# Attention in front of a dense layer: DMA transposes in and out, one score block over four banks, and v pooled by GpSimd, from pair 16 on

## The chip, the cores and the metric

The kernel runs on one core of one Trainium2 chip. The metric is the device time of one execution in microseconds (us). Every experiment is given as the median of its executions, and as a ratio to executions of the kernel before on the same chip in the same rounds.

The engines are PE (TensorE matmuls; PEld its weight loads), ACT (ScalarE), DVE (VectorE), POOL (GpSimd) and SP, whose queue here issues every DMA.

## The reference

Eight batches, eight heads, 576 tokens, head dimension 64. Two attentions are added: one over means of four tokens, one over a band of plus and minus three tokens. A dense layer with `h - tanh(h)` follows.

```python
q_d = q.reshape(B, H, Sd, 4, D).mean(axis=3)      # the same for k and v
out_d = sm_attn(q_d, k_d, v_d)                    # softmax attention, 144 x 144
out_up = np.repeat(out_d, 4, axis=2)
mask = np.abs(pos[:, None] - pos[None, :]) < 4
out_local = softmax(where(mask, q k^T / 8, -1e9)) @ v
x = (out_up + out_local) as [4608, 512]
h = x @ w_in                                      # 512 -> 2048
out = (h - tanh(h)) @ w_out                       # 2048 -> 512
```

## The kernel before

Heads are worked on in 32 pairs, four pairs to a batch. As soon as a batch has filled 512 more tokens of `xT`, a dense block (128 matmuls of 512 columns) can run; there are nine. The program lists operations with durations that it assumes, orders them by a list scheduler that prefers attention and fills PE with dense work, and writes each engine's instructions in that order. On the chip the order is fixed: **an engine that reaches an instruction too early stands still, whatever else is ready.** The waits of PE shown further down are such stops.

```python
def order(self): ...     # list scheduling with the assumed ns and latencies
LAT = {"PE": 270, "ACT": 150, "DVE": 110, "POOL": 150, "SP": 50, "DMA": 1800}
```

The parts that the change touches, cut to the core (`ts` and `ox` are two PSUM banks each, `px` is `ox` seen as bf16):

```python
# q and k: PE transposes for early pairs, a DMA transpose from pair T_DMA = 14 on
op("SP", 700, dma_start_transpose(qT[s] <- qr[s]), pri=pri)
op("DMA", 2500, None, ...)
op("ACT", 600, A.copy(full[:, i] <- qT[s][:, i]))          # twice
# scores in two blocks, each with its exponentials, both in ts
op("PE", 420, s1, writes=ts)                     # 8 matmuls of the band
op("ACT", 870, exp(e1 <- ps)); op("DVE", 700, e1 *= mask)
op("PE", 380, s2, writes=ts)                     # 2 of the band, 4 pooled
op("ACT", 240, exp(e2v <- ps)); op("ACT", 560, exp(e3 <- ps)); op("DVE", 220, e2v *= mask)
# pooling v on PE for two pairs, in ox, then a cast on ACT
op("PE", 750, six matmuls pick x vw, writes=["ox"]); op("ACT", 490, vd <- ox)
# outputs, normalisation, transposes back, join
op("PE", 570, outs, writes=ox)
op("DVE", 200, reciprocal); op("DVE", 1010, ln[s] <- po * r)
op("PE", 370, back, writes=ox)                   # 7 transposes
op("ACT", 190, od <- px[1]); op("DVE", 680, xT <- px[0] + od)
```

The softmax here doesn't subtract the row's maximum and nothing guards it: scores larger than these inputs give would overflow.

## Time and profile before

| what | number | where it is read |
|---|---|---|
| PE busy | 334.3 of 357.4 us | page, part 1 |
| last join of attention | 253 us, so 104 us of dense work alone follow | groups of the join's line |
| dense matmuls | start to start 216 ns; 1152 of them are 249 us | PE timeline |
| transposes back; pooling of v | 0.37 us per pair; 0.70 per two pairs | PE timeline |
| ACT busy, 140 to 220 us | 86% | windows |

The median was 362.01 us over three executions (361.08 to 363.34); the profiled one took 359.08 us, of which 357.4 us are the span.

This is the head of the page of the kernel before: busy time and share of the span by engine, then the busy share in tenths in 40 slices of 8.9 us.

```profile
span 357.4 us, 6978 instructions
PE 334.3 (94%) x2646; PEld 173.1 (48%) x2692; DVE 219.4 (61%) x362; ACT 236.2 (66%) x406; POOL 123.9 (35%) x156
PE   7777999999999999999999999989999999999995
ACT  3686987688864988888888899974343443434421
DMA  8999999999999999798788925200100010010012
```

PE is nearly always busy, and after slice 28, where attention is over, it alone is. But busy PE time must be read with care. The Trainium skill, "Trainium Kernel Development and Optimization", section "Performance Expectations", calls matmul busy time a bad metric, because matmuls are pipelined. This trace agrees: a dense matmul is shown as 379 ns long, yet starts follow each other every 216 ns. So PE work is costed here by the spacing of starts. These rows are from the PE timeline of the kernel before (start, length, line, operation, count): transposes back, the first score block, four dense matmuls, then pooling of v and the second score block.

```profile
191.85 0.22 PE L525 MATMUL ps_ox<-ident,ln_102 128*128 128x128 bf16 x1
191.91 0.22 PE L526 MATMUL ps_ox<-ident,ln_102 128*128 128x128 bf16 x1
191.97 0.42 PE L529 MATMUL ps_ox<-ident,ln_102 120*128 120x120 bf16 x5
192.32 0.38 PE L449 MATMUL ps_ts<-qk_90 64*128 64x120 bf16 x8
192.64 1.04 PE L581 MATMUL ps_hy_529<-w_out_sb,gT_106 128*128 128x512 bf16 x4
...
194.38 0.72 PE L361 MATMUL ps_ox<-vw_82,pick 128*128 128x256 bf16 x5
194.94 0.27 PE L363 MATMUL ps_ox<-vw_82,pick 128*128 128x256 bf16 x1
195.15 0.22 PE L449 MATMUL ps_ts<-qk_90 64*128 64x96 bf16 x2
195.20 0.29 PE L464 MATMUL ps_ts<-qkd_95 64*128 64x144 bf16 x4
195.42 0.82 PE L581 MATMUL ps_hy_529<-w_out_sb,gT_106 128*128 128x512 bf16 x3
```

From 191.85 to the next start of other work is 0.47 us for the transposes back (0.37 where nothing delays it), and pooling takes from 194.38 to 195.15, 0.77 us (six times its usual spacing of 113 ns is 0.68).

Finally what PE itself waited for between 130 and 265 us (PE instruction, releaser, us in total, times, longest; the first three of 13 lines), and the busy times of all engines from 140 to 220 us:

```profile
PE ps_ts L449 <- ACT qk_91 L404: 1.8, 4, 0.6
PE ps_ts L449 <- ACT E_97 L472: 0.8, 2, 0.6
PE ps_ox L498 <- DVE E_98 L487: 0.5, 1, 0.5
```

```profile
core 0: us, PE busy (x) PEld busy (x) DVE busy (x) ACT busy (x) POOL busy (x), PEclk, DMA share, GB/s
140.00:220.00 80.00, 76.51 (x682) 40.67 (x691) 60.93 (x99) 68.81 (x111) 39.52 (x44) 1.00 0.82 165
```

PE waits before the first score block, for the copies of q and k on ACT (L404). ACT is 86% busy there (68.81 of 80).

### The profile page before, as it was taken

How to read it: one execution, taken by the hardware profiler on the slowest of the kernel's cores; microseconds unless marked ns; L12 is line 12 of the kernel's file. 1: busy time of each engine (PE TensorE's matmuls, PEld its weight loads, DVE VectorE, ACT ScalarE, POOL GpSimd, SP SyncE). 2: the span in 40 equal slices, each digit the busy share in tenths (PEclk: the TensorE clock that was granted, in tenths of full speed). 3: DMA queues.
4: the chain of work that ended last, by engine and by line, in shares of the span. 5: the costliest groups of instructions: out<-in, count | busy, mean ns of one | idle time of the engine just before them, and what ended most of it. 6: DMA issues, size and time to landing. Idle time of an engine off the chain costs nothing.

```text
span 357.4 us, 6978 instructions
## 1 busy us (share of the span) xinstructions
PE 334.3 (94%) x2646; PEld 173.1 (48%) x2692; DVE 219.4 (61%) x362; ACT 236.2 (66%) x406; POOL 123.9 (35%) x156
## 2 busy tenths in 40 slices
PE   7777999999999999999999999989999999999995
PEld 3454455555545454545555454445444444444442
DVE  5786775869976576867887778676443334434300
ACT  3686987688864988888888899974343443434421
POOL 7654666576542346444654446420000000000000
PEclk9899999999999999999999999999999999999999
DMA  8999999999999999798788925200100010010012
GB/s 199 226 390 304 258 253 253 212 235 273 242 217 165 214 184 227 172 171 176 155 211 184 214 64 97 64 0 31 56 34 29 29 61 30 29 61 29 29 67 82
DMA packets 86128, 52.94 MB, mean 148 GB/s; under 512 B 65103, under 2 KB 77391, under 8 KB 86095
## 3 DMA queue, kind: packets, MB, share of 16 engines
q1 hardware_dynamic: 86094, 52.50, 66.3%
q8 instruction: 21, 0.34, 0.4%
q14 instruction: 13, 0.10, 0.1%
HBM read 37.74 MB, written 9.44 MB: 132 GB/s over the span
## 4 chain that ended last, share of the span: by engine, by line
PE 65%; ACT 11%; DMA 10%; DVE 6%; issue 5%; POOL 2%; SPq 1%; POOLq 0%; ACTq 0%; DVEq 0%
PE ps_hy_530 L581 7%; PE ps_hy_530 L554 7%; PE ps_hy_529 L554 7%; PE ps_hy_528 L554 7%; PE ps_hy_527 L581 7%; PE ps_hy_529 L581 7%; PE ps_hy_527 L554 6%; PE ps_hy_528 L581 5%; ACT qk_91 L404 4%; DMA vst_80<-in_v_dram 3%; DMA qkn_73<-in_q_dram 3%; ACT qk_90 L404 2%; PE ps_ox L498 2%; DMA vst_81<-in_v_dram 2%; PE ps_ox L361 2%
## 5 line engine op out<-in xcount | busy, mean ns | idle before, releaser
L554 PEld LDWEIGHTS <-w_in_sb 128*128 128x128 bf16 x576 | 52.7, 98 | 58.8 <-issue 2.2
L581 PEld LDWEIGHTS <-gT_105 128*128 128x128 bf16 x320 | 29.2, 98 | 31.6
L581 PEld LDWEIGHTS <-gT_106 128*128 128x128 bf16 x256 | 23.8, 98 | 27.6
L431 POOL TENSOR_TENSOR half<-qk_91 128x576 f32<-128x576 bf16 x16 | 19.2, 1203 | 34.5 <-ACT qk_91 L404 26.4
L431 POOL TENSOR_TENSOR half<-qk_90 128x576 f32<-128x576 bf16 x14 | 16.1, 1149 | 37.6 <-ACT qk_90 L404 31.7
L404 ACT COPY qk_90<-qT_92 128x576 bf16<-128x576 bf16 x18 | 21.0, 1180 | 0.0
L404 ACT COPY qk_91<-qT_93 128x576 bf16<-128x576 bf16 x18 | 20.7, 1188 | 0.0
L581 PE MATMUL ps_hy_527<-w_out_sb,gT_105 128*128 128x512 bf16 x78 | 20.4, 379 | 0.2 <-issue 0.2
L581 PE MATMUL ps_hy_528<-w_out_sb,gT_105 128*128 128x512 bf16 x78 | 20.3, 379 | 0.3 <-issue 0.3
L581 PE MATMUL ps_hy_529<-w_out_sb,gT_105 128*128 128x512 bf16 x75 | 20.1, 379 | 0.3
L581 PE MATMUL ps_hy_530<-w_out_sb,gT_105 128*128 128x512 bf16 x77 | 19.4, 379 | 0.3 <-issue 0.2
L515 DVE TENSOR_TENSOR ln_101<-ps_ox,r_99 128x896 bf16<-128x896 f32 x16 | 17.4, 1089 | 0.4
L472 ACT ACTIVATE E_97<-ps_ts 128x960 bf16<-128x960 f32 x16 | 15.8, 988 | 1.9 <-PE ps_ts L449 1.9
L581 PE MATMUL ps_hy_530<-w_out_sb,gT_106 128*128 128x512 bf16 x63 | 16.7, 379 | 0.3 <-issue 0.2
L581 PE MATMUL ps_hy_527<-w_out_sb,gT_106 128*128 128x512 bf16 x62 | 16.7, 379 | 0.0
L581 PE MATMUL ps_hy_528<-w_out_sb,gT_106 128*128 128x512 bf16 x60 | 16.1, 379 | 0.3 <-issue 0.2
L581 PE MATMUL ps_hy_529<-w_out_sb,gT_106 128*128 128x512 bf16 x61 | 16.0, 379 | 0.1
L475 DVE TENSOR_TENSOR E_97<-E_97,mask 128x960 bf16<-128x960 bf16 x16 | 13.5, 844 | 3.5 <-ACT E_97 L472 3.2
L515 DVE TENSOR_TENSOR ln_102<-ps_ox,r_100 128x896 bf16<-128x896 f32 x14 | 15.2, 1088 | 0.4
L472 ACT ACTIVATE E_98<-ps_ts 128x960 bf16<-128x960 f32 x14 | 13.7, 976 | 2.4 <-PE ps_ts L449 1.7
L475 DVE TENSOR_TENSOR E_98<-E_98,mask 128x960 bf16<-128x960 bf16 x16 | 13.5, 844 | 2.1 <-ACT E_98 L472 2.1
L554 PE MATMUL ps_hy_527<-xT_66,w_in_sb 128*128 128x512 bf16 x35 | 13.3, 380 | 1.4 <-DVE xT_69 L534 1.2
(220 smaller groups left out, 867.2 us busy)
## 6 DMA issues: line engine op xcount, KB each, us to landing
out_dram<-y_110 SPq DMA_DIRECT2D x12, 256.0 KB, 2.3
out_dram<-y_111 SPq DMA_DIRECT2D x12, 256.0 KB, 3.0
out_dram<-y_112 SPq DMA_DIRECT2D x12, 256.0 KB, 2.1
qkn_72<-in_q_dram SPq DMA_DIRECT2D x8, 288.0 KB, 7.3
qkn_72<-in_k_dram SPq DMA_DIRECT2D x8, 288.0 KB, 7.3
qkn_73<-in_q_dram SPq DMA_DIRECT2D x8, 288.0 KB, 4.7
qkn_73<-in_k_dram SPq DMA_DIRECT2D x8, 288.0 KB, 5.5
qkn_74<-in_q_dram SPq DMA_DIRECT2D x8, 288.0 KB, 6.7
```

Source lines behind the costliest of these rows:

```text
L361: T.matmul(pv[:, 0, :], pick[:, t, :], vw[w][:, :, t, 0:64], start=(t == 0), stop=(t == NT - 1))
L404: op("ACT", 600, lambda i=i: A.copy(out=full[:, i].rearrange("p (g a) -> p g a", a=A6), in_=qT[s][:, i].rearrange("p a g -> p g a")), read ...
L431: eng.tensor_tensor(out=half, in0=four[:, :, :, 0:2], in1=four[:, :, :, 2:4], op=ALU.add)
L472: op("ACT", 870, lambda: A.activation(out=e1, in_=ps[:, :, 0:480], func=AF.Exp, scale=SCALE), reads=ts, writes=[("E", s, 0)], pri=pri)
L475: op("DVE", 700, lambda: V.tensor_tensor(out=e1, in0=e1, in1=mask[:, 0:480].unsqueeze(1).to_broadcast([128, 2, 480]), op=ALU.mult), reads= ...
L498: T.matmul(po[:, hh, 65 * t:65 * t + 65], E[s][:, c:c + 128], vw[w][:, 2 * jj + hh, t, :], start=True, stop=True)
L515: op("DVE", 1010, lambda: V.tensor_tensor(out=ln[s].rearrange("p n (h d) -> p h n d", d=D), in0=blocks[:, :, :, 0:64], in1=r[s].unsqueeze( ...
L554: T.matmul(ps_hy[slot], w_in_sb[:, dc, fc * 128:(fc + 1) * 128], xT[dc][:, kb * 512:kb * 512 + 512], start=(dc == 0), stop=(dc == N_DC - 1))
L581: T.matmul(ps_hy[slot], gT[g][:, fc, ts * 128:ts * 128 + 128], w_out_sb[:, fc, :], start=(fc == 0), stop=(fc == N_FF - 1))
```

## The change

From pair 16 on: v is pooled by two additions on GpSimd, from a second load of v in rows of four tokens; the scores are one PE block over the four banks of `ts` and `ox`; the outputs go back through a DMA transpose, and DVE or GpSimd joins the two attentions in SBUF. DMA transposes of q and k start at pair 16, not 14, come first in the DMA queue and are planned as shorter. The v buffers go from 6 to 5 to make room. Some smaller parts of the diff also touch earlier pairs (padding of `E` and `qkd`, one of the seven transposes back on 16 rows instead of 128).

```diff
-    NQKN, NVST, NVW = 4, 6, 3
+    NQKN, NVST, NVW = 4, 5, 3
+    v4 = fixed("v4", [72, 2, 2, 4 * D], FP32, 2)
+    vp = fixed("vp", [72, 2, 2, D + 1], BF16, 2)
+    lT = fixed("lT", [128, 7, 128], BF16, 2)
     ...
+        op("POOL", 1150, a1, reads=[("v4", s)], writes=["v2"], pri=10 * p - 12)
+        op("POOL", 750, a2, reads=["v2"], writes=[("vp", s)], pri=10 * p - 12)
     ...
-               writes=[("qT", s), ("qTq", s)], pri=pri)
-            op("DMA", 2500, None, ...
+               writes=[("qT", s), ("qTq", s)], pri=-50)
+            op("DMA", 1300, None, ...
     ...
+        if new:
+            op("PE", 620, s12, reads=qks + [("qkd", s)], writes=ts + ox, pri=pri)
     ...
+        if p >= X_DMA:
+            op("SP", 600, lambda: nc.sync.dma_start_transpose(
+                out=lT[s], in_=ln[s].rearrange("p n c -> p (n c)")), ..., pri=-50)
+            ...                                # the planned DMA, the definition of join
+            P.choice([("DVE", 850, lambda: join(V)), ("POOL", 1450, lambda: join(GP))],
+                     reads=[("lT", s)], writes=[("x", b, j)], pri=pri)
+            return
     ...
-    M2_FIRST, T_DMA = 16, 14
+    M2_FIRST, T_DMA, X_DMA, NEW = 16, 16, 16, 16
```

More of the change, by code (lines that the diff above doesn't have):

```diff
@@ L193 @@
     mask = fixed("mask", [128, 576], BF16)
-    warm = fixed("warm", [128, 512], BF16)
     xT = [fixed(f"xT{j}", [128, NTOK], BF16) for j in range(NP)]
@@ L205 @@
     half = fixed("half", [128, 2, G, 2], FP32)
-    qkd = fixed("qkd", [128, 2, G], BF16, 2)
-    E = fixed("E", [128, 1728], BF16, 2)
+    qkd = fixed("qkd", [128, 344], BF16, 2)
+    v4 = fixed("v4", [72, 2, 2, 4 * D], FP32, 2)
+    v2 = fixed("v2", [72, 2, 2, 2 * D], FP32)
+    vp = fixed("vp", [72, 2, 2, D + 1], BF16, 2)
+    E = fixed("E", [128, 1840], BF16, 2)
+    lT = fixed("lT", [128, 7, 128], BF16, 2)
+    warm = lT[0].rearrange("p n c -> p (n c)")[:, 0:512]
     r = fixed("r", [128, 2, 7], FP32, 2)
@@ L351, in prep_v, with load_v4, issue, pool_v4 @@
                  writes=[("vw", w, jj)], pri=10 * p - 12)
+    def load_v4(p):
+        b, h0, s = p // NP, 2 * (p % NP), p % 2
+        src = v[b, h0]
+        def issue():
+            nc.sync.dma_start(
+                out=v4[s].rearrange("p h w c -> p (h w) c"),
+                in_=bass.AP(tensor=src.tensor, offset=src.offset,
+                            ap=[[4 * D, 72], [72 * 4 * D, 4], [1, 4 * D]]))
+        load(700, issue, [("v4", s)], 1100, -30)
+    def pool_v4(p):
+        s = p % 2
+        def a1():
+            GP.tensor_tensor(out=v2, in0=v4[s][:, :, :, 0:128],
+                             in1=v4[s][:, :, :, 128:256], op=ALU.add)
+        def a2():
+            GP.tensor_tensor(out=vp[s][:, :, :, 0:64], in0=v2[:, :, :, 0:64],
+                             in1=v2[:, :, :, 64:128], op=ALU.add)
+        op("POOL", 1150, a1, reads=[("v4", s)], writes=["v2"], pri=10 * p - 12)
+        op("POOL", 750, a2, reads=["v2"], writes=[("vp", s)], pri=10 * p - 12)
     def pool_v(hb):
@@ L399, in attention @@
                reads=[("qr", s, 0), ("qr", s, 1)],
-               writes=[("qT", s), ("qTq", s)], pri=pri)
-            op("DMA", 2500, None, reads=[("qTq", s), ("qr", s, 0), ("qr", s, 1)],
+               writes=[("qT", s), ("qTq", s)], pri=-50)
+            op("DMA", 1300, None, reads=[("qTq", s), ("qr", s, 0), ("qr", s, 1)],
                writes=[("qT", s)], pri=pri)
@@ L435, in add2 @@
             with nc.allow_low_precision("pooled q and k"):
-                eng.tensor_tensor(out=qkd[s], in0=half[:, :, :, 0],
+                eng.tensor_tensor(out=qkd[s][:, 0:2 * G].rearrange("p (i g) -> p i g", i=2),
+                                  in0=half[:, :, :, 0],
                                   in1=half[:, :, :, 1], op=ALU.add)
@@ L444, in attention, with score @@
         sc = ps.rearrange("p n c -> p (n c)")
-        def score(t, hh, c):
+        def score(t, hh, c, sc=sc):
             rows = slice(64 * hh, 64 * hh + 64)
@@ L455, in s1, with s2 @@
                     score(t, hh, 512 * hh + QW * t)
-        def s2():
+        def s2(sc=sc, step=16):
             for hh in range(2):
-                score(4, hh, 512 * hh)
+                score(4, hh, 512 * hh, sc)
             for i in range(2):
@@ L463, in s2, with s12 @@
                     c = 512 * hh + 96 + G * i
-                    T.matmul(sc[:, c:c + G], qkd[s][rows, 1, 16 * i:16 * i + 128],
-                             qkd[s][rows, 0, :], start=True, stop=True)
+                    k0 = G + step * i
+                    T.matmul(sc[:, c:c + G], qkd[s][rows, k0:k0 + 128],
+                             qkd[s][rows, 0:G], start=True, stop=True)
+        def s12():
+            s1()
+            s2(po.rearrange("p n c -> p (n c)"), 72)
         qks = [("qk", s, i) for i in range(2)]
         yield
-        op("PE", 420 * cold, s1, reads=qks, writes=ts, pri=pri)
+        new = p >= NEW
+        ps2, ts2 = (po, ox) if new else (ps, ts)
+        if new:
+            op("PE", 620, s12, reads=qks + [("qkd", s)], writes=ts + ox, pri=pri)
+        else:
+            op("PE", 420 * cold, s1, reads=qks, writes=ts, pri=pri)
         e1 = E[s][:, 0:960].rearrange("p (h c) -> p h c", h=2)
@@ L479, in attention @@
         yield
-        op("PE", 380 * cold, s2, reads=qks + [("qkd", s)], writes=ts, pri=pri)
+        if not new:
+            op("PE", 380 * cold, s2, reads=qks + [("qkd", s)], writes=ts, pri=pri)
         op("ACT", 240, lambda: A.activation(
-            out=e2v, in_=ps[:, :, 0:96], func=AF.Exp, scale=SCALE),
-           reads=ts, writes=[("E", s, 1)], pri=pri)
+            out=e2v, in_=ps2[:, :, 0:96], func=AF.Exp, scale=SCALE),
+           reads=ts2, writes=[("E", s, 1)], pri=pri)
         op("ACT", 560, lambda: A.activation(
-            out=e3, in_=ps[:, :, 96:384], func=AF.Exp, scale=SCALE / 16.0),
-           reads=ts, writes=[("E", s, 2)], pri=pri)
+            out=e3, in_=ps2[:, :, 96:384], func=AF.Exp, scale=SCALE / 16.0),
+           reads=ts2, writes=[("E", s, 2)], pri=pri)
         op("DVE", 220, lambda: V.tensor_tensor(
@@ L500, in outs @@
                 for half in range(2):
-                    c = 1152 + 288 * hh + 16 * half
+                    c = 1152 + 288 * hh + 128 * half
                     o = 65 * (NT + half)
                     for i in range(2):
+                        vv = vp[s][:, hh, i, :] if new else vd[w][:, i, 2 * jj + hh, :]
                         T.matmul(po[:, hh, o:o + 65],
-                                 E[s][:, c + G * i:c + G * i + 128],
-                                 vd[w][:, i, 2 * jj + hh, :],
-                                 start=(i == 0), stop=(i == 1))
+                                 E[s][0:vv.shape[0], c + G * i:c + G * i + 128],
+                                 vv, start=(i == 0), stop=(i == 1))
         P.fresh.add(len(P.ops))
         op("PE", 570 * cold, outs,
-           reads=[("E", s, 0), ("E", s, 1), ("E", s, 2), ("vw", w, jj), ("vd", w)],
+           reads=[("E", s, 0), ("E", s, 1), ("E", s, 2), ("vw", w, jj),
+                  ("vp", s) if new else ("vd", w)],
            writes=ox, pri=pri)
@@ L525, in back @@
             T.transpose(px[1][:, 0:128], ln[s][:, 5, :], ident)
-            T.transpose(px[1][:, 16:144], ln[s][:, 6, :], ident)
+            T.transpose(px[1][:, 128:144], ln[s][0:16, 6, :], ident[0:16, 0:16])
             for t in range(NT):
@@ L530, in back, with join @@
                             ident[0:n, 0:n])
+        if p >= X_DMA:
+            op("SP", 600, lambda: nc.sync.dma_start_transpose(
+                out=lT[s], in_=ln[s].rearrange("p n c -> p (n c)")),
+               reads=[("ln", s)], writes=[("lT", s), ("lTq", s)], pri=-50)
+            op("DMA", 1000, None, reads=[("lTq", s), ("ln", s)],
+               writes=[("lT", s)], pri=pri)
+            pool = lT[s][:, 5:7, :].rearrange("p n c -> p (n c)")[:, 0:G]
+            def join(eng):
+                x0 = xT[j][:, b * S:b * S + 480]
+                eng.tensor_tensor(
+                    out=x0.rearrange("p (t g a) -> p t g a", t=4, a=4),
+                    in0=lT[s][:, 0:4, 0:QW].rearrange("p t (g a) -> p t g a", a=4),
+                    in1=pool[:, 0:120].rearrange("p (t g) -> p t g", t=4)
+                    .unsqueeze(3).to_broadcast([128, 4, 30, 4]), op=ALU.add)
+                x1 = xT[j][:, b * S + 480:(b + 1) * S]
+                eng.tensor_tensor(
+                    out=x1.rearrange("p (g a) -> p g a", a=4),
+                    in0=lT[s][:, 4, 0:96].rearrange("p (g a) -> p g a", a=4),
+                    in1=pool[:, 120:144].unsqueeze(2).to_broadcast([128, 24, 4]),
+                    op=ALU.add)
+            P.choice([("DVE", 850, lambda: join(V)), ("POOL", 1450, lambda: join(GP))],
+                     reads=[("lT", s)], writes=[("x", b, j)], pri=pri)
+            return
         op("PE", 370 * cold, back, reads=[("ln", s)], writes=ox, pri=pri)
@@ L651 @@
            writes=[("vd", i)], pri=-96)
+    for i in range(2):
+        op("DVE", 70, lambda i=i: V.memset(E[i][:, 1728:1840], 0.0),
+           writes=[("E", i, 2)], pri=-94)
     op("DVE", 1200, c_pick, reads=["group"], writes=["pick"], pri=-95)
@@ L692 @@
     made = 0
+    for i in range(2):
+        op("DVE", 70, lambda i=i: V.memset(qkd[i][:, 288:344], 0.0),
+           writes=[("qkd", i)], pri=-94)
+        op("DVE", 70, lambda i=i: V.memset(vp[i][:, :, :, 64:65], 4.0),
+           writes=[("vp", i)], pri=-94)
     work = [attention(p) for p in range(NPAIR)]
@@ L697 @@
     for p in range(NPAIR):
-        if p % 2 == 0:
+        if p % 2 == 0 and p < NEW:
             pool_v(p // 2)
@@ L710 @@
         load_next()
+        if NEW <= p + 1 < NPAIR:
+            pool_v4(p + 1)
+        if NEW <= p + 3 < NPAIR:
+            load_v4(p + 3)
         if p % NP == NP - 1:
```

## The prediction

> **What bounds the kernel now.** TensorE. The page gives PE 334.3 of 357.4 us busy. After the last attention pair (last join at 252 us) only dense work is left, four matmuls per 0.86 us (chain of waits): 105 us of the 9 dense blocks is a pure PE tail. At pair 16 (about 132 us) some 300 of 1152 dense matmuls are done and 512 are ready, so PE has filler throughout. Attention pace (about 7.3 us per pair, DMA queue's timeline) matters only where PE waits in order for it. The waits show some 7.5 us of PE idle between 120 and 250 us. ACT (85 to 90% busy, windows) and the DMA engines (share about 0.95 from 120 to 200) stand close behind.
>
> **What goes, per pair from 16 on**, by spacing in the PE timeline rather than busy time, which overlaps:
> - transposes back: seven matmuls, 0.37 us
> - pooling v on PE: 0.70 us per two pairs, 0.35
> - two score blocks (0.32 and about 0.28) become one; three interruptions of dense work vanish, some of which cost 0.1 to 0.2 us ("issue" waits before weight loads). I put 0.15 here.
>
> So 0.87 us per pair, 14 us over 16 pairs, all on the bounding engine. Pairs 14 and 15 return to PE transposes: plus 1.2 us. ACT loses the 0.29 us copy of od and half of vd's 0.59 us cast per pair, about 9 us, and some slow copies (1.18 to 0.64 us): another 2 us.
>
> **What comes.** POOL: two additions on 72 partitions, by elements from the present 1.2 and 0.75 us ones, about 1.7 us per pair; POOL is half idle. The join takes SBUF inputs, about 0.75 us on DVE as before. The Trainium skill, "SBUF — State Buffer", section "SBUF: two separate sides", says GpSimd and a DVE operation with two SBUF inputs block each other on a shared port pair; the trace agrees: the same mask product takes 0.64 to 1.19 us. More of that, off the critical path. DMA, per pair: 295 KB more loads (estimate 1 us of 16 engines) and an output transpose (a present one takes about 2.1 us of 16 engines from 220 to 240 us, 4.6 us to landing; the new one estimate 1.7): share 1.0 to 1.2, as at 60 to 100 us. SP works in order and transposes hold it 1.25 to 3.1 us each, so loads queue longer. The four-bank score block must wait until the previous pair's normalisation frees its banks: score, exponentials (2.0 us), outputs, normalisation (1.3) plus queueing, an estimated 7 to 8 us loop, about today's pace.
>
> **Net.** Attention ends at 252 to 262 us, equal or slightly later, with more dense work done by then; the backlog never runs out. Gain 14, less 1.2, less a little for new in-order PE waits: 12.5, so 349.5 us, range 343 to 356. Chances: faster by over 2% 0.77, same 0.18, slower 0.05.
>
> **Right if:** PE idle from 130 to 260 us stays under 10 us; the tail after the last join shrinks to 85 to 95 us; attention PE work per pair falls from 1.95 to about 1.15 us; POOL busy grows by 25 to 30 us; landing of input transposes rises to 5 to 6 us.
>
> **Wrong if:** the DMA queue sets the pace and PE stands at the score blocks waiting for late input transposes (over 1 us per pair), or the bank loop exceeds 9 us per pair, or the shorter v prefetch (5 buffers) delays the DMA-bound first 70 us.

## The result, and the profile after

The changed kernel took 348.24 us (median of four, 346.70 to 348.94) against 361.77 (four), a ratio of 0.961 with a 95% interval of 0.957 to 0.966. Executions over 1.5% slower than the fastest of the same kernel are left out of the means. The predicted 349.5 us was 1.3 us off. Its page:

```profile
span 346.3 us, 6847 instructions
PE 328.0 (95%) x2556; PEld 163.5 (47%) x2556; DVE 223.8 (65%) x362; ACT 224.8 (65%) x382; POOL 169.9 (49%) x210
PE   6787989999999999999999999899999999999995
ACT  4585886768978768787878778599753434343411
DMA  8999999999999998999999999645231000100021
```

PE stays full, GpSimd gains 46 us, and the DMA engines are busy to slice 25, not 23, and nearer to full from slice 17 on. The PE timeline around one pair shows one score block in place of two:

```profile
195.70 0.39 PE L478 MATMUL ps_ts<-qk_88 64*128 64x120 bf16 x8
195.92 0.21 PE L478 MATMUL ps_ox<-qk_88 64*128 64x96 bf16 x2
195.97 0.29 PE L494 MATMUL ps_ox<-qkd_93 64*128 64x144 bf16 x4
196.19 0.39 PE L619 MATMUL ps_hy_539<-xT_65,w_in_sb 128*128 128x512 bf16 x1
```

It takes 0.49 us from its first start to the next dense matmul. Then PE's waits from 130 to 265 us and the same stretch of busy times as before:

```profile
PE ps_ox L538 <- DVE E_100 L527: 1.5, 3, 0.7
PE ps_ox L538 <- DVE E_100 L514: 0.4, 2, 0.2
PE ps_ox L538 <- DVE E_101 L514: 0.4, 1, 0.4
```

```profile
140.00:220.00 80.00, 77.78 (x610) 37.83 (x609) 62.72 (x90) 61.27 (x96) 62.39 (x72) 1.00 1.13 233
```

The waits for ACT before the score blocks are gone. In their place PE now waits inside the output block (L538) for the mask products on DVE (L514, L527). ACT fell from 68.81 to 61.27 us, POOL rose from 39.52 to 62.39, and the DMA share from 0.82 to 1.13.

**An account of PE.** I split the span of each profiled execution into PE work and PE idle. Work is the number of weight loads of a kind (all are recorded, some matmuls are not) times the usual spacing of starts of that kind: 216 ns for a dense matmul (and for the 28 warming ones at the start), 54 for a transpose back, 113 for one of pooling, 32 in an output block, 43 for an input transpose, 23 on average for scores, which start in twos 4 ns apart. The 216 ns agrees with the Trainium skill, "TensorE: Matmul & The Clock Gate", section "Wait — 56ns, not 53.3ns?", which gives 215.7 ns for 512 columns. Idle is the rest; it holds the start (15 us of the first 30), what a reduced clock costs, and 4 us at the end.

| profiled execution | span | PE work | of it back / pooling / input transposes | PE idle | idle, late | last join at |
|---|---|---|---|---|---|---|
| before | 357.4 | 313.8 | 12.1 / 10.8 / 7.2 | 43.6 | 21.6 | 253.1 |
| after | 346.3 | 303.3 | 6.0 / 5.4 / 8.3 | 42.9 | 17.4 | 260.9 |

So 10.5 of the 11.1 us between these two executions is PE work that is no longer done. Idle from 130 us on fell from 18.5 to 13.7 us, and idle before that rose from 25.1 to 29.2; in this run the clock was lower in the first slices, 0.83 against 0.91 in the first 20 us. The medians differ by 13.5 us; the profiled execution of the kernel before was one of its fast ones, and the 2.4 us in between lie within its own spread.

The column "idle, late" leaves out a part that only blurs the comparison. In all fourteen profiles PE's first 850 weight loads are of the same kinds in the same order, and yet PE idle up to there, 94 to 99 us into the span, runs from 22.0 us (before) to 27.6 us; it is 25.5 us in the changed kernel. "Idle, late" is the idle time after these 850. It fell by 4.2 us, so with 10.5 us of work the change is worth 14.7 us after that point, against 13.5 by the medians. Whether the smaller v buffer has a part in the idle time before it was not tested.

### The profile page after: what moved, and what is told of

Same layout as the page of the kernel before. It is cut to its first block, busy times and chain, and to the rows that moved or that the text cites. A ratio compares the mean times of both kernels' runs of the same rounds, so it can differ in the third digit from the quotient of the medians.

```text
span 346.3 us, 6847 instructions
## 1 busy us (share of the span) xinstructions
PE 328.0 (95%) x2556; PEld 163.5 (47%) x2556; DVE 223.8 (65%) x362; ACT 224.8 (65%) x382; POOL 169.9 (49%) x210
## 4 chain that ended last, share of the span: by engine, by line
PE 69%; DVE 10%; ACT 9%; issue 3%; DMA 3%; POOL 2%; SPq 1%; ACTq 0%; POOLq 0%; DVEq 0%
PE ps_hy_540 L646 8%; PE ps_hy_538 L619 8%; PE ps_hy_539 L619 7%; PE ps_hy_541 L646 7%; PE ps_hy_538 L646 7%; PE ps_hy_539 L646 6%; PE ps_hy_540 L619 6%; PE ps_hy_541 L619 6%; PE ps_ox L538 3%; DVE qr_87 L416 2%; PE ps_ts L478 2%; DMA qkn_73<-in_k_dram 2%; PE ps_ox L545 2%; PE ps_ts L442 2%; PE ps_ox L389 2%
## 5 line engine op out<-in xcount | busy, mean ns | idle before, releaser
L646 PEld LDWEIGHTS <-gT_110 128*128 128x128 bf16 x320 | 30.2, 98 | 34.5
L646 PEld LDWEIGHTS <-gT_111 128*128 128x128 bf16 x256 | 24.0, 98 | 27.4
L646 PE MATMUL ps_hy_539<-w_out_sb,gT_110 128*128 128x512 bf16 x80 | 20.7, 379 | 0.0
L646 PE MATMUL ps_hy_540<-w_out_sb,gT_110 128*128 128x512 bf16 x80 | 20.4, 379 | 0.0
L646 PE MATMUL ps_hy_538<-w_out_sb,gT_110 128*128 128x512 bf16 x80 | 20.4, 379 | 0.0
L646 PE MATMUL ps_hy_541<-w_out_sb,gT_110 128*128 128x512 bf16 x80 | 20.1, 379 | 0.0
L432 ACT COPY qk_89<-qT_91 128x576 bf16<-128x576 bf16 x16 | 18.7, 1193 | 0.0
L432 ACT COPY qk_88<-qT_90 128x576 bf16<-128x576 bf16 x16 | 18.4, 1188 | 0.0
L556 DVE TENSOR_TENSOR ln_106<-ps_ox,r_104 128x896 bf16<-128x896 f32 x16 | 17.4, 1090 | 0.5
L646 PE MATMUL ps_hy_540<-w_out_sb,gT_111 128*128 128x512 bf16 x64 | 16.9, 379 | 0.0
L646 PE MATMUL ps_hy_541<-w_out_sb,gT_111 128*128 128x512 bf16 x64 | 16.8, 379 | 0.0
L646 PE MATMUL ps_hy_539<-w_out_sb,gT_111 128*128 128x512 bf16 x64 | 16.6, 379 | 0.0
L646 PE MATMUL ps_hy_538<-w_out_sb,gT_111 128*128 128x512 bf16 x64 | 16.4, 379 | 0.0
L514 DVE TENSOR_TENSOR E_101<-E_101,mask 128x960 bf16<-128x960 bf16 x16 | 13.1, 820 | 3.9 <-ACT E_101 L511 3.7
L514 DVE TENSOR_TENSOR E_100<-E_100,mask 128x960 bf16<-128x960 bf16 x16 | 13.6, 847 | 2.8 <-ACT E_100 L511 2.8
```

Source lines behind the costliest of these rows:

```text
L432: op("ACT", 600, lambda i=i: A.copy(out=full[:, i].rearrange("p (g a) -> p g a", a=A6), in_=qT[s][:, i].rearrange("p a g -> p g a")), read ...
L514: op("DVE", 700, lambda: V.tensor_tensor(out=e1, in0=e1, in1=mask[:, 0:480].unsqueeze(1).to_broadcast([128, 2, 480]), op=ALU.mult), reads= ...
L556: op("DVE", 1010, lambda: V.tensor_tensor(out=ln[s].rearrange("p n (h d) -> p h n d", d=D), in0=blocks[:, :, :, 0:64], in1=r[s].unsqueeze( ...
L646: T.matmul(ps_hy[slot], gT[g][:, fc, ts * 128:ts * 128 + 128], w_out_sb[:, fc, :], start=(fc == 0), stop=(fc == N_FF - 1))
```

## The experiments

Theory: PE always has dense work ready, so the time is PE work plus PE idle, and 0.71 us of work per pair left PE. Rivals: (A) the 11 us taken off ACT did it; (B) the other order of issue, with its waits, did it.

| run | edit of the changed kernel | median, us | ratio to before (95%) | PE work | PE idle | idle, late | last join |
|---|---|---|---|---|---|---|---|
| (after) | none | 348.2 | 0.961 (0.957 to 0.966) | 303.3 | 42.9 | 17.4 | 260.9 |
| x_pe_back | outputs back by PE | 355.5 | 0.981 (0.974 to 0.989) | 309.4 | 44.7 | 18.5 | 273.2 |
| old_scores_pool | scores and pooling as before | 360.6 | 0.993 (0.983 to 1.002) | 308.8 | 51.7 | 24.8 | 242.0 |
| pe_dose | 12.5 us of empty PE work | 357.3 | 0.986 (0.978 to 0.995) | 315.9 | 39.3 | 14.6 | 269.4 |
| act_dose | 9 us of empty ACT work | 348.4 | 0.963 (0.955 to 0.971) | 303.3 | 43.1 | 18.6 | 261.0 |
| scores_only | v pooled on PE | 352.6 | 0.974 (0.965 to 0.982) | 308.8 | 41.8 | 15.9 | 251.5 |
| gp_pool_only | scores in two blocks | 352.1 | 0.972 (0.964 to 0.980) | 303.3 | 47.2 | 21.4 | 255.8 |
| pace_dose | 20 us more on GpSimd | 358.1 | 0.987 (0.978 to 0.996) | 303.3 | 52.5 | 26.4 | 270.9 |
| hints_back | planning figures as before | 354.7 | 0.978 (0.969 to 0.988) | 303.3 | 47.1 | 24.5 | 270.2 |
| less_dma | second v load almost gone (wrong result) | 358.7 | 0.987 (0.980 to 0.995) | 303.3 | 53.7 | 27.5 | 258.2 |
| all12 | all but the input transposes from pair 12 | 355.1 | 0.980 (0.973 to 0.986) | 300.5 | 52.6 | 26.4 | 273.0 |
| join_dve | joins on DVE only | 345.6 (344.3 without a slow one) | 0.950 (0.941 to 0.959) | (slow run) | | | |
| join_dve_again | the same kernel | 346.3 | 0.957 (0.952 to 0.962) | 303.3 | 42.3 | 16.3 | 260.2 |

All were correct but less_dma. The kernel before took 361.4 to 362.3 us (medians of fast executions) beside these runs. Work, idle and last join are those of each profiled execution. Against the changed kernel, work and late idle together differ by what the medians differ by, to about 1 us, in every row that has them (old_scores_pool: 5.5 and 7.4 us, by the medians 12.4); total idle does so less well.

### Is it PE, or ACT?

**x_pe_back** puts the transposes back on PE.

```diff
-    M2_FIRST, T_DMA, X_DMA, NEW = 16, 16, 16, 16
+    M2_FIRST, T_DMA, X_DMA, NEW = 16, 16, 32, 16
```

> The changed kernel with the output transposes put back on PE (seven matmuls and a copy on ACT per pair, no output DMA). Theory (the time is PE work plus PE idle, and PE has a backlog of dense work): 16 pairs x 0.37 us = 6 us come back, 354 us (352 to 356), with PE work by counts and spacing 6 us up on the changed kernel. Rival A (the gain came from ACT, which lost 11 us): 16 x 0.29 us of copies come back, at most 4.6 us and less, as ACT is no longer full. Rival B (the gain is the fewer in-order waits or the new order of issue): no change beyond 2 us.

It gave 355.5 us, 7.3 more, with 6.1 us more work and 1.8 us more idle. Rival A allows at most 4.6.

**pe_dose** and **act_dose** add work to one engine and leave the order alone.

```diff
         def outs():
+            if new:                            # ahead of the output matmuls
+                junk = po[:, 0].bitcast(BF16)
+                for z in range(14):
+                    T.transpose(junk[:, 128 * (z % 4):128 * (z % 4) + 128], ident, ident)
```

> The changed kernel with 14 transposes of the identity added ahead of the output matmuls of each pair from 16 on, overwritten afterwards, in unchanged order on every engine: about 14 x 0.053 = 0.75 us of PE work per pair, 12 us in all, nothing on any other engine. Theory: 12 us slower, 360 us (358 to 362). Rivals A and B: PE has room, so it takes at most half, 354 us or less.

```diff
+        def exp3():
+            A.activation(out=e3, in_=ps2[:, :, 96:384], func=AF.Exp, scale=SCALE / 16.0)
+            if new:
+                for z in range(2):
+                    A.copy(out=od[s], in_=ps2[:, z, 96:240])
```

> The changed kernel with two copies of 144 elements from PSUM (0.29 us each) added on ACT after the third exponential of each pair from 16 on, order unchanged: 16 x 0.58 = 9.3 us more on ACT, as much as the change took off it. Theory: ACT is off the critical path, 348 to 350 us. Rival A: most of 9 us comes back, 354 to 358 us.

The dose on ACT cost nothing clear of the noise (348.4 us): rival A falls. The dose on PE cost 9.1 us, less than the 12 expected and 0.7 us under the range given, but well over the rivals' 6. The account says why: work rose by 12.5 us, and idle fell by 3.6 (late idle by 2.8), because PE came later to the waits in the output blocks and found the mask products done: by spacing PE lost 0.3 us there, against 4.2 in the changed kernel. So in this run a microsecond of PE work cost 0.73 us.

### Scores and pooling

**old_scores_pool** undoes both.

```diff
-    M2_FIRST, T_DMA, X_DMA, NEW = 16, 16, 16, 16
+    M2_FIRST, T_DMA, X_DMA, NEW = 16, 16, 16, 32
```

> The changed kernel with the scores in two blocks and v pooled on PE as before, output and input transposes by DMA. Theory: 16 x 0.34 us of pooling on PE and 16 x about 0.1 us of a further block come back, 7 us, so 355 us (353 to 357). Rival A: 8 casts of 0.59 us, at most 4.7 us. Rival B: less than 2 us. A fourth possibility, that the wait of the four-bank block for its banks costs something, would make this smaller than 7 us.

It cost 12.4 us by the medians where 7 were expected. Work rose by 5.5 as foreseen; idle by 8.8 (late idle by 7.4), which was not. So two runs split the pair, with separate thresholds for the two parts:

```diff
+    M2_FIRST, T_DMA, X_DMA, NEW, NEWV = 16, 16, 16, 16, 32     # scores_only
+    M2_FIRST, T_DMA, X_DMA, NEW, NEWV = 16, 16, 16, 32, 16     # gp_pool_only
```

> Score blocks merged from pair 16 on as in the change, but v pooled on PE as before (no second load of v); transposes as in the change. Undoing scores and pooling together cost 12 us, of which 5.5 is PE work of pooling and 9 is PE idle. Theory 1 (the merged block is what removed the idle, by fewer interruptions and one wait instead of two): only the 5.4 us of pooling come back, PE idle stays within 2 us of the changed kernel's 43: 353 to 355 us. Theory 2 (pooling on PE, with its wait for the banks of the outputs and its cast on ACT, makes the idle): 358 to 361 us.

> v pooled by GpSimd from the second load as in the change, but the scores of pairs 16 on in two blocks over two banks as before. PE work as in the changed kernel (303 us). Theory 1: PE idle rises by 6 to 9 us, 354 to 357 us. Theory 2: idle stays near 43 us, 348 to 350 us. If both give about half, the two act together.

With merged scores and pooling on PE (scores_only), the 5.5 us of pooling are back and idle is no higher: 352.6 us, 0.4 under the range of theory 1. With GpSimd pooling and two score blocks (gp_pool_only), work is that of the changed kernel, but idle is 4.3 us up (late idle 4.0): 352.1 us, between the ranges of the two theories. So **pooling on GpSimd pays through work, the merged score block through idle**. By spacing, the time lost between dense matmuls and a score block after 130 us was 6.2 us before, 4.9 in gp_pool_only, and 1.5 in both kernels with merged blocks. Alone the two are worth 4.4 and 3.9 us, undone together 12.4; the missing 4 us are idle of old_scores_pool, where PE waited 4.4 us at score blocks for ACT's copies of q and k. Why these waits are longer there than in gp_pool_only was not settled.

That run also shows that an early end of attention does not make a fast kernel: with the last join earliest of all, at 242.0 us, it is the slowest, while the changed kernel ends attention 7.8 us later than the kernel before and is 13.5 us faster.

### Pace, plan and waits

**pace_dose** doubles the first GpSimd addition and tells the plan so.

```diff
-        op("POOL", 1150, a1, reads=[("v4", s)], writes=["v2"], pri=10 * p - 12)
+        op("POOL", 2400, a1_twice, reads=[("v4", s)], writes=["v2"], pri=10 * p - 12)
```

> The changed kernel with the first GpSimd addition of the pooling of v done twice (1.27 us more on GpSimd per pair, 20 us in all), and told so to the ordering, which so plans attention slower: attention gets slower, PE work is the same. Theory (PE has a backlog of dense work, so attention pace is off the critical path as long as the order of PE's instructions expects it): last join 5 to 20 us later, time within 3 us of 348. Rival (attention pace bounds): 355 us or more.

358.1 us: my expectation failed. PE work was the same, idle 9.6 us higher. But the waits do not say that attention's pace bounds; 9.0 of the 12.0 us that PE waits from 130 to 275 us are for mask products:

```profile
PE ps_ox L541 <- DVE E L530: 6.4, 9, 1.5
PE ps_ox L541 <- DVE E L517: 2.6, 2, 2.2
```

And the mask products themselves were slower, though nothing was added to DVE. Groups of DVE from 130 to 260 us (count, busy us, mean ns, idle before and its releaser), first the changed kernel, then pace_dose:

```profile
L514 DVE TENSOR_TENSOR E_100<-E_100,mask 128x960 bf16<-128x960 bf16 x8 | 7.6, 956 | 2.1 <-ACT E_100 L511 2.0
L514 DVE TENSOR_TENSOR E_101<-E_101,mask 128x960 bf16<-128x960 bf16 x8 | 6.9, 857 | 2.9 <-ACT E_101 L511 2.8
L527 DVE TENSOR_TENSOR E_100<-E_100,mask 128x192 bf16<-128x192 bf16 x8 | 3.7, 462 | 0.0
```

```profile
L517 DVE TENSOR_TENSOR E<-E,mask 128x960 bf16<-128x960 bf16 x15 | 19.0, 1268 | 7.4 <-ACT E L514 7.4
L530 DVE TENSOR_TENSOR E<-E,mask 128x192 bf16<-128x192 bf16 x15 | 9.2, 611 | 0.0
```

The large product went from 907 ns (mean of 956 and 857) to 1268, the small one to 611. That is what the Trainium skill, "SBUF — State Buffer", section "SBUF: two separate sides", describes: a GpSimd instruction that reads SBUF and a DVE instruction with two SBUF inputs hold a shared port pair in turn. The traces agree. In the fourteen profiles together, the 150 products of this size that no GpSimd instruction overlapped took 0.64 to 0.66 us, all of them; the others took up to 3.76 us. After 130 us, 12 of 16 are overlapped in pace_dose (mean 1.42 us) and 13 of 16 in the changed kernel (0.97 us). So a dose on GpSimd is not only a change of pace; this run does not test what it was made for.

**less_dma** was to test the pace without touching an engine.

```diff
+            if p >= NEW + 2:
+                nc.sync.dma_start(out=v4[s][:, 0, 0, 0:64], in_=...)   # a sixteenth of the row
+                return
-        load(700, issue, [("v4", s)], 1100, -30)
+        load(700 if p < NEW + 2 else 300, issue, [("v4", s)], 1100 if p < NEW + 2 else 100, -30)
```

> The changed kernel with the second load of v cut to a sixteenth from pair 18 on (pairs 18 and up then pool old values: a wrong result on purpose) and the ordering told that it is cheap. Frees the saturated DMA queue by an estimated 1 us per pair: a clean test of attention pace, which touches no engine's work. Rival (attention pace bounds the time): last join some 10 us earlier and time down by 5 us or more. Theory (PE has backlog; pace is off the path): last join earlier, 245 to 258 us, time within 2.5 us of 348.

Both theories missed: 358.7 us, with less DMA and the same work. Attention was hardly faster (last join 258.2 us; input transposes every 8.0 us against 8.6), so the pace was not what was bought. The plan, told that a load is cheap, had changed the order, so this run is no clean test of pace either. By spacing PE lost 10.7 us at and in the output blocks after 130 us, against 4.2 in the changed kernel, again with waits for the mask products. DVE came to them later: from pair 18 on the large product began 1.20 us after its exponentials on average, against 0.54 us. What in the order did that was not followed up.

**hints_back** changes the order alone.

```diff
-               writes=[("qT", s), ("qTq", s)], pri=-50)
-            op("DMA", 1300, None, ...
+               writes=[("qT", s), ("qTq", s)], pri=pri)
+            op("DMA", 2500, None, ...
```

> The changed kernel with the planning figures of the input transposes put back (2500 ns and the pair's priority in the DMA queue, instead of 1300 ns and the first place): the same instructions in another order. Theory: the same PE work, so within 3 us of 348, any difference being PE idle. Rival B (the gain is in the order): 353 us or more.

354.7 us, more than the 3 us that I allowed: rival B holds in part. The same instructions in another order cost some 6 us (4.2 us of idle in the profiled execution, 7.1 of late idle; it was the fastest of its four). Part of it may be clock: in that execution, after waits of 0.72 and 0.96 us, the granted clock stood at 0.50 from 213.9 to 220.7 us, and the other three had a lower mean clock still (0.971 to 0.975, against 0.990). Not run was the other side: the kernel before with the new planning figures alone. So, as far as these runs show, the gain needs the work removed **and** an order that fits.

### More of it, and a repair

**all12** starts outputs, scores and pooling at pair 12.

```diff
-    M2_FIRST, T_DMA, X_DMA, NEW = 16, 16, 16, 16
+    M2_FIRST, T_DMA, X_DMA, NEW = 16, 16, 12, 12
```

> The changed kernel with output transposes, merged scores and GpSimd pooling from pair 12 on instead of 16 (input transposes by DMA still from 16). Theory: 4 more pairs lose 0.37 + 0.34 us of PE work, 2.9 us, and some idle; against it stands that the DMA engines are at a share of 1.2 there and that less dense work is ready: 345 to 348 us. If DMA sets the pace there and PE has no backlog, 350 us or more with PE idle up between 80 and 130 us.

Work fell by 2.8 us as expected, but the time rose to 355.1 us: the expectation failed. The added idle is not between 80 and 130 us, where I had looked for it, but just after. Windows of this run:

```profile
136.00:140.00 4.00, 3.56 (x28) 1.46 (x26) 4.00 (x4) 4.00 (x6) 3.92 (x4) 1.00 0.97 219
140.00:144.00 4.00, 1.71 (x26) 1.35 (x27) 2.91 (x5) 1.04 (x2) 2.69 (x4) 0.74 1.28 223
144.00:148.00 4.00, 1.53 (x22) 1.08 (x22) 3.32 (x4) 3.01 (x5) 4.00 (x4) 0.50 1.16 256
148.00:152.00 4.00, 4.00 (x28) 1.63 (x26) 3.56 (x6) 1.15 (x2) 3.56 (x5) 0.50 1.17 232
152.00:156.00 4.00, 4.00 (x25) 1.92 (x24) 2.97 (x7) 3.55 (x8) 1.45 (x2) 0.98 1.16 198
```

And the PE timeline inside them, with the idle time before a row and its releaser in brackets:

```profile
141.19 0.30 PE L538 MATMUL ps_ox<-vw,E 128*128 128x65 bf16 x4 [1.63 <-DVE E L514]
144.26 0.27 PE L478 MATMUL ps_ox<-qk 64*128 64x96 bf16 x2 [1.01 <-DVE ln L556]
146.69 0.40 PE L538 MATMUL ps_ox<-vw,E 128*128 128x65 bf16 x4 [1.93 <-DVE E L514]
```

These are three in-order waits of 1.0 to 1.9 us, two for mask products and one for the normalisation that frees the banks of the four-bank score block. The granted clock (PEclk, the third column from the end) fell to half at 141.9 us, after the first of them and one more of 0.34 us (L527, not shown); the other two came while it was at half already, and it stayed there until 152 us. The same happened once more, at 217.0 us, after one wait of 1.84 us for a mask product. Even 148 to 152 us, where PE is never idle, runs at 0.50, so two of these four microseconds are lost to the clock. The Trainium skill, "TensorE: Matmul & The Clock Gate", section "Why this matters for your kernels", warns of idle gaps over about 3 us. The trace agrees on the kind of effect, but here shorter gaps were enough. No dense matmul runs between these blocks, from 139.5 to 148 us. Whether none was ready or the order only had none there was left open.

**join_dve** takes the GpSimd joins (11 of 16 in the changed kernel) to DVE, to give the mask products their port back.

```diff
-            P.choice([("DVE", 850, lambda: join(V)), ("POOL", 1450, lambda: join(GP))],
+            P.choice([("DVE", 850, lambda: join(V))],
```

> The changed kernel with the join of the output transposes only on DVE (in the changed kernel GpSimd does 11 of 16). After the dose on GpSimd slowed DVE's mask products and PE waited for them, this takes GpSimd work away: 11 x 1.5 us. Theory (what is left of new PE waits comes from GpSimd blocking DVE's mask products): mask products of 960 elements after 130 us shorter than the 0.91 us mean of the changed kernel, PE idle ahead of and inside the output blocks down from 4.2 us to 2 or less, time 345 to 348 us. Rival (DVE, 75% busy, is the short one): DVE gets 11 x 0.95 us more, masks come later, 349 to 352 us.

345.6 us (344.3 without a slow one) at a ratio of 0.950 (0.941 to 0.959). Its profile fell on a slow run, so it ran again:

> The kernel of join_dve once more, because its profile fell in the slow state and its interval (0.941 to 0.959) touches that of the changed kernel (0.957 to 0.966). If the join on DVE is a gain of its own: ratio to the kernel before 0.945 to 0.956, 343 to 346 us, and PE waits for mask products in the output blocks at 2 us or less after 130 us (4.2 us in the changed kernel). If it was luck of the runs: 0.958 to 0.965, 347 to 350 us.

346.3 us, 0.957 (0.952 to 0.962), between the two outcomes that I had set apart. PE's waits from 130 to 265 us in that run:

```profile
PE ps_ox L538 <- DVE E L527: 0.8, 2, 0.5
PE ps_ox L478 <- DVE ln L556: 0.7, 2, 0.5
PE ps_ox L538 <- DVE E L514: 0.4, 1, 0.4
```

Waits for masks fell from 2.3 to 1.2 us (by spacing, from 4.2 to 2.4 us; 2 or less was expected), the large product to 818 ns, and idle after 130 us from 13.7 to 11.7. The kernel is faster than the changed one by 4.0 us in the first run and 1.9 us in the second, by medians of fast executions. It clearly beats the kernel before; against the changed kernel the intervals of the second run overlap (0.952 to 0.962 against 0.957 to 0.966), so that step is likely and not proven.

## Why the prediction was right, point by point

- **What bounds** (PE, with dense work always ready): right. 10.5 us in the profiles are PE work, and 4.2 us late idle; ACT work of the size that was removed could be put back for nothing clear of the noise (act_dose), PE work could not (x_pe_back, pe_dose).
- **Removed work**, 0.37 and 0.35 us per pair: measured 0.38 and 0.34 (16 pairs: 6.0 and 5.4 us by the account). The two extra pairs of input transposes were put at 1.2 us and measured 1.0.
- **Interruptions**, 0.15 us per pair or 2.4 us: under-sized. The merged score block alone was worth 3.9 us (gp_pool_only), and together with pooling's removal the idle that it saves reached 8.8 us (old_scores_pool; 7.4 of late idle).
- **New waits**: put down as "a little". They are 4.2 us by spacing at the output blocks (0.6 before), for mask products, not for late input transposes. This and the item above have opposite signs, so the sum came out right partly because two terms that were too small cancelled. That part is luck.
- **Attention's end**, 252 to 262 us: 260.9. The tail was 85.4 us (85 to 95 predicted), PE idle from 130 us to that join 9.1 us (under 10 predicted), landing of input transposes 5.2 us by median (the trace tells 8 of 16), from 4.6 (5 to 6 predicted).
- **PE work of attention per pair**, from 1.95 to 1.15: the fall is 0.71 by the account, from 1.61 to 0.90. I had counted gaps into the work.
- **GpSimd**, 25 to 30 us more: wrong, 46. The two additions took 1.27 and 0.73 us, and 11 of 16 joins, which I had put on DVE, ran on GpSimd. This mattered more than "off the critical path" says: join_dve, which undoes a part of it, is likely the faster kernel.
- **"Attention pace matters only where PE waits in order for it"**: right as worded, but I took it too lightly. The order set by the planning figures alone was worth about 6 us (hints_back), and the sum of the prediction has no term for it. That the new order was a good one was not foreseen either.
- **"About today's pace"** for the loop over the four banks: wrong. By the issue of the input transposes a pair took 6.8 us from pair 16 on before (I had read 7.3) and 8.6 after. Time did not follow it. What sets the 8.6 us was not settled; less DMA moved it only to 8.0.

## What to carry to other kernels

Where one engine has a backlog, count what leaves that engine by the spacing of its instructions, and check the claim by putting the same amount back on each engine in turn. In a statically ordered program, take the in-order waits as a second budget: a merged block can save waits, and a new order can cost as much as the work it saves. Before moving two-input work to GpSimd, look at which DVE products of two SBUF inputs the bounding engine waits for.

## What the Trainium skill lacked or had wrong

- "TensorE: Matmul & The Clock Gate" warns of single idle gaps of about 3 us or more and mentions frequent micro-idles, but gives no size for these. After 130 us the granted clock fell to 0.50 five times in these profiles (all12 at 141.9 and 217.0 us, hints_back at 213.9, less_dma at 167.2 and 218.4), for 3.4 to 10.2 us. In the 3.4 us before each fall PE was busy for 1.4 to 1.8 us, and the longest single gap was 0.82 to 1.84 us. A gap of 2.22 us in pace_dose, which ended at 235.3 us, brought no fall. A measure for short gaps near each other is missing.
- "SBUF — State Buffer" names the shared port pair but gives no time for a product of this kind. Here a 128x960 product of two SBUF inputs took 0.64 to 0.66 us when no GpSimd instruction overlapped it, and 0.64 to 1.20 us in the kernel before over all; its mean after 130 us went from 0.91 in the changed kernel to 1.27 us in pace_dose, where GpSimd got one more addition of 1.27 us per pair and the order changed too.
- "DMA: Bandwidth & Descriptors" gives a bandwidth for DMA transposes but no time to landing for a small one from SBUF to SBUF on this chip. Here one of 96 x 1536 elements landed 4.6 us after issue (median before) and 5.2 us in the busier queue after, and held the issuing queue for 1.2 to 3.9 us.
